# Feed-forward work listed in pieces of two blocks; pooled scores head by head, pooled products with V in blocks of 48 queries

## The chip, the core and the metric

The kernel runs on one core of a Trainium2 chip. The metric is the device time of one execution in microseconds (us); of several executions the median is taken. The core's engines run side by side, each through its own list of instructions in order: TensorE (PE; its weight loads are shown as PEld), VectorE (DVE), ScalarE (ACT), GpSimd (POOL), and SyncE (SP), which here issues every DMA.

## The reference

Eight sequences of 576 positions with 8 heads of 64 go through two attentions whose sum goes through a normalisation and a feed-forward layer of 2048 inner units; everything is float32.

```python
q_d = q.reshape(B, H, Sd, 4, D).mean(axis=3)          # Sd = 144; k_d, v_d alike
out_up = np.repeat(sm_attn(q_d, k_d, v_d), 4, axis=2)  # pooled attention, 144 x 144 scores a head
mask = np.abs(pos[:, None] - pos[None, :]) < 4
out_local = softmax(where(mask, scale * q @ k.T, -1e9)) @ v
x = (out_up + out_local)                               # 4608 rows of 512
xn = (x - mean) / sqrt(var + 1e-6) * g_ln
out = x + relu(xn @ w_ch1) @ w_ch2                     # 512 -> 2048 -> 512
```

## The kernel before

**Three streams of work.** The *local* attention takes 40 windows (5 a sequence), each with 8 heads: scores `ls` (L573, L587), a transpose of the attention `lt` (L622), products with V `lv` (L643). The *pooled* attention takes each sequence in two halves of four heads (`pooled_half`), each in two pairs of heads (`pooled_pair`): 32 pairs, of which the four of sequence 0 (`own`) have forms of their own. The *feed-forward* layer takes 18 chunks of 256 rows; the 2048 inner units are 8 pairs of two blocks of 128 (`ffn(c, p)`). For each block, `up(fi)` makes 12 matmuls into `h` (L1048) and `down(fi)` 6 into `acc` (L1071): inputs and weights are split into a high and a low float32r part, and three of the four products are kept. There are 288 `up` and 288 `down` pieces.

**A pooled pair before (not of sequence 0).** `turn_qk` transposes Q and K of both heads (`gq`, L791). `turn_qk_out` copies Q of each head into its own rows and columns of `qbdg`, a block-diagonal tile whose other parts stay zero, and K into `ktg` (L800, L804). `scores` then needs three matmuls, of 128 rows and 96 columns, 48 queries of both heads at once, over 144 keys (`gs`, L818). `largest` is one maximum over 96 x 432 and one small product on DVE (L822, L823), `exps` three activations (L831). `turn_a` transposes the attention in two halves of the keys, three transposes of 96 columns each (`gt`, L837), each copied out by `turn_a_out` (L847). `times_v` is eight matmuls of 72 x 72 by 65 columns (`gv`, L854), `divided` follows on DVE, and `keep` writes the result to DRAM in one DMA (L877).

**Array tiles.** Matmuls of `ls` and `lv` have 64 rows and 64 columns, and stand on four 64 x 64 tiles of TensorE's 128 x 128 array, those of L428 (sequence 0's transposes, `lq`, `lk`) on two tiles of 128 x 64. All other matmuls use the whole array.

**What sets the order.** Nothing is ordered by hand. Each piece of work is a task of `Plan`: engine, assumed duration, the tasks that it depends on, a due time, and the "rooms" (buffers, PSUM banks among them) that it takes and gives. A task is never split. `Plan.order` simulates the engines and, among the tasks that can start, takes the one that is due first. Due times follow a pace: chunk `c` is due at `T0 + CHUNK * c`, so `CHUNK` (56) scales the dues of attention too. The order that comes out is what each engine executes.

Of the kernel before, what the change touches and what calls it, by code (L numbers as in the profile page):

```python
# [139 lines left out]
def attention_then_ffn(  # L140
# [72 lines left out]
    qbdg = [const.tile([P, 3, 2 * GB], F32, name=f"qbdg{i}") for i in range(2)]  # L213
# [56 lines left out]

    T0 = 35
    C1 = 5
    CHUNK = 56
    PACE = CHUNK / NPR

    def chunk_at(c):
# [45 lines left out]
    def act(n, sbuf=False):  # L322
        return (0.155 if sbuf else 0.14) + n / 1430.0
# [404 lines left out]
    def pooled(b):  # L728
        due0 = pooled_at(b, 0)
        add = plan.add  # L730
        for hg in range(2):
            pooled_half(b, hg)

    def pooled_half(b, hg):
        add = plan.add
        i = 2 * b + hg
        x = SimpleNamespace(m={})
        vd = vds[hg]
        ready = {}
        own = b < NPB  # L740
        if own:
            ready["q"], ready["k"] = list(gsum_done[b, hg, "q"]), list(gsum_done[b, hg, "k"])
        for nm, src in (("v", v),) if own else (("q", q), ("k", k), ("v", v)):
            for half in range(2):
                key = (nm, half)
                due = pooled_at(b, 2 * hg) - (8.0 if nm == "v" else 14.0)
# [28 lines left out]
                ready.setdefault(nm, []).append(t)  # L775
        for pr in range(2):
            pooled_pair(b, hg, pr, x, ready)

    def pooled_pair(b, hg, pr, x, ready):
# [2 lines left out]
        due = pooled_at(b, 2 * hg + pr)  # L782
        y = SimpleNamespace(at={})
        own = b < NPB
        bd, vd = qbdg[pr], vds[hg]

        def turn_qk():
            y.pt = psa(f"gq{i}_{pr}")[:, : 2 * SD].rearrange("p (t g) -> p t g", t=2)
# [17 lines left out]
        def arrange():
            for h2 in range(2):
                hs = slice(64 * h2, 64 * h2 + 64)
                nc.scalar.copy(
                    bd[hs, :, h2 * GB : (h2 + 1) * GB],  # L810
                    gsum[b, hg, "q"][hs, pr].rearrange("p (c g) -> p c g", c=3),
                )
            y.kt = gsum[b, hg, "k"][:, pr]

        def scores():
            y.ps = psa(f"gs{i}_{pr}")[: 2 * GB, : 3 * SD].rearrange("p (c g) -> p c g", c=3)
            for c in range(3):
                nc.tensor.matmul(y.ps[:, c], lhsT=bd[:, c], rhs=y.kt, start=True, stop=True)  # L818

        def largest():  # L820
            y.mx = work.tile([2 * GB, 3], F32, tag="gmx", bufs=4, name=f"gmx{i}_{pr}")
# [18 lines left out]
                )  # L840

        def turn_a_out(kh):
            if own:
                y.at[kh] = unit([GH, 2, SD], f"agt{i}_{pr}_{kh}")
            else:
                y.at[kh] = work.tile([GH, 2, SD], F32, tag=f"agt{kh}", name=f"agt{i}_{pr}_{kh}")
            nc.scalar.copy(y.at[kh].rearrange("p h (c g) -> p c h g", c=3), y.pa[kh])  # L847

        def times_v():
            y.pv = psa(f"gv{i}_{pr}")[:GH, : 4 * (D + 1)].rearrange("p (q h e) -> p q h e", q=2, h=2)  # L850
            for h2 in range(2):
                for qh in range(2):
                    for kh in range(2):
                        nc.tensor.matmul(  # L854
                            y.pv[:, qh, h2], lhsT=y.at[kh][:, h2, qh * GH : (qh + 1) * GH],
                            rhs=vd[:, kh, 2 * pr + h2], start=kh == 0, stop=kh == 1,
                        )

        def divided():
            r = work.tile([GH, 2, 2], F32, tag="gr", bufs=4, name=f"gr{i}_{pr}")  # L860
# [19 lines left out]
            )  # L880

        if b < NPB:
            t = add("ACT", 0.43, arrange, ready["q"] + ready["k"] + [lastg.s[pr]], due - 8.0)
        else:
            t = add("PE", 0.25, turn_qk, ready["q"] + ready["k"], due - 8.0, take=A, give=(("u", 2),) if pr else ())
            t = add("ACT", 0.52, turn_qk_out, (t, lastg.s[pr]), due - 8.0, give=A)
        t = lastg.s[pr] = add(
            "PE", 0.73, scores, (t,), due - 6.0, take=A, give=(("u", 2),) if b < NPB and pr else ()
        )
        t = add("DVE", 0.7, largest, (t,), due - 5.0)  # L890
        ex = add("ACT", 0.79, exps, (t, None if own else lastg.t), due - 5.0, take=U if own else (), give=A)
        outs = []
        for kh in range(2):
            t = lastg.t = add("PE", 0.25, lambda kh=kh: turn_a(kh), (ex,), due - 3.0, take=A,
                                give=U if own and kh else ())
            outs.append(add("ACT", act(288), lambda kh=kh: turn_a_out(kh), (t, None if own else lastg.v), due - 3.0,
                            take=U if own else (), give=A))
        t = add("PE", 1.04, times_v, outs + ready["v"], due - 1.0, take=A, give=(("u", 2),) if own else ())
        lastg.v = lastg.vd[hg] = t
        t = add("DVE", 0.68, divided, (t,), due, take=U if b < NPB and pr == 0 else (), give=A)  # L900
        od_done.append(t)
# [134 lines left out]
    def ffn(c, p):  # L1036
# [48 lines left out]
            nc.sync.dma_start(out_f[n * P : (n + 1) * P], xt[n])  # L1085

        ups = []
        for fi in range(2):
            ups.append(
                add("PE", 1.44, lambda fi=fi: up(fi),  # L1090
                    xt_done[c] + [wdone[1, 2 * p + fi]] + ups[-1:] + [f1_last.get(c)], due + 0.1 * fi,
                    take=() if fi else A, give=rooms("xh", "xh", "xlo", "xlo") if p == NPR - 1 and fi else ())
            )
# [4 lines left out]
        for fi in range(2):  # L1098
            prev = add(
                "PE", 1.38, lambda fi=fi: down(fi), (t, wdone[2, 2 * p + fi], prev),  # L1100
                due + (2 * PACE if c < 2 else PACE) * (OFF0 if c < 2 else 2) + 0.1 * fi,
                take=(("a", TPC),) if p == 0 and fi == 0 else (), give=rooms("hh", "hl") if fi else (),
            )
        f2_done[c] = prev
        if p == NPR - 1:
# [65 lines left out]
```

## Time and profile before

| | us |
|---|---|
| Median of 3 runs | 1056.92 |
| Lowest, highest | 1055.81, 1063.01 |
| The profiled execution | 1053.27 |
| Its span, first to last instruction | 1051.3 |

| Engine | busy us | share of the span |
|---|---|---|
| PE | 1034.3 | 98% |
| PEld | 928.9 | 88% |
| DVE | 514.0 | 49% |
| ACT | 309.8 | 29% |
| POOL | 251.0 | 24% |

Matmuls are pipelined, and one that is recorded as 0.40 us long can be followed by the next after 0.23 us. So a busy PE tells little, and the cost of matmuls is read here from the **starts** in the timeline: from the start of a group to the start of what follows. In the timeline `64*64` stands for rows and columns of the array, `64x65` for what is written; a float32 matmul shows as two records, a transpose and a float32r matmul as one. A few per cent of the records are missing.

### The profile page before, as it was taken

The page shows a single profiled execution, that of the slowest core. Times are in us where ns is not written, and L with a number is a line of the kernel's source. Part 1 is how long each engine was busy: PE and PEld are TensorE (multiplying, and loading weights), DVE is VectorE, ACT ScalarE, POOL GpSimd, SP SyncE. Part 2 cuts the span into 40 slices and gives each one's busy share as a digit, 9 for nine tenths or more (in the row PEclk, how much of TensorE's full clock was granted, in tenths as well). Part 3 has the DMA queues.
Part 4 walks back from the last instruction along what each step waited for, and adds up shares of the span by engine and source line. Part 5 has one row for each costly group of instructions (what it writes and reads, how often), then busy time and mean ns, then how long its engine had stood idle before and what let it go on. Part 6 is the DMA issues. An engine that isn't in the chain of part 4 may idle for free.

```text
span 1051.3 us, 24104 instructions
## 1 busy us (share of the span) xinstructions
PE 1034.3 (98%) x9450; PEld 928.9 (88%) x9450; DVE 514.0 (49%) x1301; ACT 309.8 (29%) x846; POOL 251.0 (24%) x272
## 2 busy tenths in 40 slices
PE   9999899999999999999999999999999999999998
PEld 8887798988899989989898989899989899888997
DVE  7799976343444435444434443544434444534211
ACT  6676533232212222221323222222221222221110
POOL 4213552214014320231404150141401300000000
PEclk9999999999999999999999999999999999999999
DMA  7897474434344534343434443253442443301000
GB/s 177 251 283 210 136 176 95 114 64 114 61 101 91 133 75 110 62 124 56 91 94 96 104 97 99 47 134 67 114 87 69 92 88 65 80 11 52 7 21 21
DMA packets 283702, 104.38 MB, mean 99 GB/s; under 512 B 229789, under 2 KB 270493, under 8 KB 283589
## 3 DMA queue, kind: packets, MB, share of 16 engines
q1 hardware_dynamic: 283589, 102.84, 40.8%
q8 instruction: 75, 1.23, 0.5%
q14 instruction: 38, 0.31, 0.1%
HBM read 82.58 MB, written 11.80 MB: 90 GB/s over the span
## 4 chain that ended last, share of the span: by engine, by line
PE 83%; DVE 6%; DMA 5%; SPq 2%; issue 1%; POOL 1%; ACT 1%; ACTq 0%; DVEq 0%; POOLq 0%
PE h L1048 34%; PE acc L1071 33%; PE gv L854 3%; DMA s<-in_moe_w_ch_dram 2%; PE gs L818 2%; PE lv L643 2%; PE ls L587 2%; DVE cva L370 2%; PE lt L622 1%; PE px L975 1%; PE gt L837 1%; DVE lo L383 1%; SPq L714 1%; DMA x<-xl 1%; DVE cva L367 1%
## 5 line engine op out<-in xcount | busy, mean ns | idle before, releaser
L1071 PE MATMUL acc<-hi,hl 128*128 128x512 f32 x576 | 237.2, 412 | 0.6 <-DVE hl L1059 0.5
L1071 PE MATMUL acc<-lo,hh 128*128 128x512 f32 x576 | 227.4, 395 | 0.0
L1071 PE MATMUL acc<-hi,hh 128*128 128x512 f32 x576 | 225.2, 391 | 0.0
L1059 DVE SCALAR_TENSOR_TENSOR hl<-h,hh 128x512 fp32r<-128x512 f32 x144 | 98.9, 687 | 250.7 <-ACT hh L1055 222.0
L1055 ACT ACTIVATE hh<-h 128x512 fp32r<-128x512 f32 x144 | 86.2, 599 | 430.3 <-PE h L1048 363.5
L1048 PE MATMUL h<-xh,lo 128*128 128x256 f32 x1152 | 193.6, 291 | 0.2 <-DVE lo L383 0.2
L1048 PE MATMUL h<-xh,hi 128*128 128x256 f32 x1152 | 185.2, 283 | 0.0
L1048 PE MATMUL h<-xlo,hi 128*128 128x256 f32 x1152 | 185.0, 283 | 0.0
L1048 PEld LDWEIGHTS h<-xh,lo 128*128 128x128 f32 x1152 | 169.0, 190 | 17.4 <-DVE lo L383 0.4
L1048 PEld LDWEIGHTS h<-xlo,hi 128*128 128x128 f32 x1152 | 158.9, 192 | 0.0
L1048 PEld LDWEIGHTS h<-xh,hi 128*128 128x128 f32 x1152 | 158.6, 191 | 0.0
L948 POOL TENSOR_TENSOR x<-x,up 128x512 f32<-128x512 f32 x32 | 41.2, 1287 | 386.3 <-DMA x<-xl 208.1
L1071 PEld LDWEIGHTS acc<-hi,hh 128*128 128x128 f32 x576 | 108.5, 188 | 25.0
L1071 PEld LDWEIGHTS acc<-hi,hl 128*128 128x128 f32 x576 | 109.2, 190 | 16.9 <-DVE hl L1059 1.2
L1071 PEld LDWEIGHTS acc<-lo,hh 128*128 128x128 f32 x576 | 109.5, 190 | 12.7 <-DVE lo L383 0.3
L982 ACT ACTIVATE xh<-px,gain 128x128 fp32r<-128x128 f32 x144 | 43.7, 372 | 72.7 <-PE px L975 42.4
L992 DVE SCALAR_TENSOR_TENSOR xlo<-px,gain,xh 128x128 fp32r<-128x128 f32 x144 | 43.1, 345 | 39.1 <-ACT xh L982 38.6
L1079 DVE SCALAR_TENSOR_TENSOR x<-acc,x 128x512 f32<-128x512 f32 x36 | 24.7, 689 | 39.8 <-PE acc L1071 39.8
L831 ACT ACTIVATE ag<-gs,gmx 96x144 f32<-96x144 f32 x96 | 29.0, 374 | 41.9 <-DVE gmx L823 34.4
L370 DVE SCALAR_TENSOR_TENSOR cva<-s,cva 128x256 int32<-128x256 int32 x64 | 40.0, 665 | 1.1
L854 PEld LDWEIGHTS gv<-vd,agt 72*72 72x72 f32 x512 | 37.1, 145 | 1.2
L854 PE MATMUL gv<-vd,agt 72*72 72x65 f32 x512 | 37.9, 228 | 0.0
(196 smaller groups left out, 1106.9 us busy)
## 6 DMA issues: line engine op xcount, KB each, us to landing
s<-in_moe_w_ch_dram SPq DMA_DIRECT2D x64, 256.0 KB
vwin<-in_v_dram SPq DMA_DIRECT2D x160, 64.0 KB
out_dram<-x SPq DMA_DIRECT2D x36, 256.0 KB
qr<-in_q_dram SPq DMA_DIRECT2D x264, 32.0 KB
kr<-in_k_dram SPq DMA_DIRECT2D x264, 32.0 KB
up<-ud SPq DMA_DIRECT2D x28, 256.0 KB
x<-xl SPq DMA_DIRECT2D x74, 42.0 KB
ud<-od SPq DMA_DIRECT2D x32, 72.0 KB
```

The source lines that it names most:

```text
L370: nc.vector.scalar_tensor_tensor(out=a, in0=x.raw[i].rearrange("p (n two) -> p n two", two=2)[:, :, 0], scalar=29, in1=a, op0=ALU.logical_ ...
L587: nc.tensor.matmul(x.ps[par][64 * h2 : 64 * h2 + 64, pr], lhsT=x.qt[hs, 2 * pr + h2], rhs=x.kt[hs, 2 * pr + h2], start=True, stop=True,)
L831: nc.scalar.activation(y.a[:, c], y.ps[:, c], AF.Exp, scale=POOLED_SCALE, bias=y.mx[:, c : c + 1])
L854: nc.tensor.matmul(y.pv[:, qh, h2], lhsT=y.at[kh][:, h2, qh * GH : (qh + 1) * GH], rhs=vd[:, kh, 2 * pr + h2], start=kh == 0, stop=kh == 1,)
L948: nc.gpsimd.tensor_add(xt[n], xt[n], x.up)
L982: nc.scalar.activation(xh[c][i][:, k, j * P : (j + 1) * P], pxt[n][:, kc], AF.Copy, scale=gain[:, kc : kc + 1])
L992: nc.vector.scalar_tensor_tensor(out=xlo[c][i][:, k, ts], in0=pxt[n][:, kc], scalar=gain[:, kc : kc + 1], in1=xh[c][i][:, k, ts].bitcast(F ...
L1048: nc.tensor.matmul(ph[c, p][:, fi], lhsT=wt[:, kc], rhs=xx[kc // 2][:, kc % 2], start=n == 0, stop=n == 3 * KC - 1)
L1055: nc.scalar.activation(hh[c, p], ph[c, p], AF.Relu)
L1059: nc.vector.scalar_tensor_tensor(out=hl[c, p].rearrange("p c t -> p (c t)"), in0=ph[c, p].rearrange("p c t -> p (c t)"), scalar=0.0, in1=h ...
L1071: nc.tensor.matmul(acc[c][j], lhsT=lt[:, fi, ts], rhs=rt, start=p == 0 and fi == 0 and n == 0, stop=p == NPR - 1 and fi == 1 and n == 2,)
L1079: nc.vector.scalar_tensor_tensor(out=x, in0=acc[c][j], scalar=1.0 + 2.0**-23, in1=x, op0=ALU.mult, op1=ALU.add)
```

## The change

- **Feed-forward pieces.** For chunks 2 to 17, the two `up` pieces of a pair become one task (24 matmuls), and the two `down` pieces one (12 matmuls). Chunks 0 and 1 keep single pieces.
- **Pace.** `CHUNK` goes from 56 to 53.
- **Pooled scores by head** (sequences 1 to 7, 28 pairs): Q and K are copied in one activation. Each head then has its own three matmuls of 64 rows and 48 columns; the two heads stand on the diagonal 64 x 64 tiles and write two PSUM banks. The maximum, its product, the exponentials and the transposes are done once for each head: 2 maxima, 6 activations, 12 transposes of 48 columns on tiles of 64 x 128.
- **Products with V in blocks of 48 queries**: 12 matmuls instead of 8, on the two 128 x 64 column halves, one head on each. The first head's matmul takes 64 columns, so that the unused rows between the heads hold numbers too. The division works on 112 x 192 instead of 72 x 256; the result leaves in two DMAs of 256 B pieces instead of one of 512 B pieces.
- `qbdg` is still used by sequence 0; it is now cleared by a task (`clear_qbdg`) in buffers that are given back.

The core of the diff (dues, rooms and the scheduling of the pooled tasks follow from it):

```diff
-    CHUNK = 56
+    CHUNK = 53
...
+        def turn_qk_out_both():
+            y.qk = work.tile([P, 2, SD], F32, tag="ktg", bufs=2, name=f"ktg{i}_{pr}")
+            nc.scalar.copy(y.qk.rearrange("p t g -> p (t g)"), y.pt.rearrange("p t g -> p (t g)"))
+
+        def scores_by_head():
+            y.ps = [psa(f"gs{i}_{pr}_{h2}")[:, : 3 * SD].rearrange("p (c g) -> p c g", c=3) for h2 in range(2)]
+            for c in range(3):
+                for h2 in range(2):
+                    hs = slice(64 * h2, 64 * h2 + 64)
+                    nc.tensor.matmul(
+                        y.ps[h2][64 * h2 : 64 * h2 + GB, c], lhsT=y.qk[hs, 0, c * GB : (c + 1) * GB], rhs=y.qk[hs, 1],
+                        start=True, stop=True,
+                    )
...
+        def turn_a_by_head(h2):
+            hs = slice(64 * h2, 64 * h2 + GB)
...
+            for kh in range(2):
+                for c in range(3):
+                    n = (3 * kh + c) * GB
+                    nc.tensor.transpose(
+                        y.pa[h2][:, n : n + GB], y.a[hs, c, kh * GH : (kh + 1) * GH], ident[hs, hs]
+                    )
...
+        def times_v_by_third():
+            y.pv = psa(f"gv{i}_{pr}")[: 64 + GB, : 3 * (D + 1)].rearrange("p (c e) -> p c e", c=3)
+            for c in range(3):
+                for kh in range(2):
+                    for h2 in range(2):
+                        m = GB if h2 else 64
+                        c0 = (6 * h2 + 3 * kh + c) * GB
+                        nc.tensor.matmul(
+                            y.pv[64 * h2 : 64 * h2 + m, c], lhsT=y.at.rearrange("p h n -> p (h n)")[:, c0 : c0 + m], rhs=vd[:, kh, 2 * pr + h2],
+                            start=kh == 0, stop=kh == 1,
+                        )
...
+            t = lastg.qk[pr] = add("PE", 0.4, scores_by_head, (t,), due - 6.0, take=(("a", 2),))
+            exs = []
+            for h2 in range(2):
+                t1 = add("DVE", 0.78, lambda h2=h2: largest_by_head(h2), (t,), due - 5.0)
+                exs.append(add("ACT", 1.1, lambda h2=h2: exps_by_head(h2), [t1, lastg.t] + exs, due - 5.0, give=A))
...
-        t = add("PE", 1.04, times_v, outs + ready["v"], due - 1.0, take=A, give=(("u", 2),) if own else ())
+        t = add("PE", 1.04 if own else 0.5, times_v if own else times_v_by_third, outs + ready["v"], due - 1.0, take=A, give=(("u", 2),) if own else ())
...
-        for fi in range(2):
+        groups = ((0,), (1,)) if c < 2 else ((0, 1),)
+        for fs in groups:
             ups.append(
-                add("PE", 1.44, lambda fi=fi: up(fi),
+                add("PE", 1.44 * len(fs), lambda fs=fs: [up(fi) for fi in fs],
...
-                "PE", 1.38, lambda fi=fi: down(fi), (t, wdone[2, 2 * p + fi], prev),
+                "PE", 1.38 * len(fs), lambda fs=fs: [down(fi) for fi in fs],
...
+    bd_done = plan.add("DVE", 0.6, clear_qbdg, (), 0.0, take=(("u", 2),))
```

**Two places in the order of TensorE.** The first is the pooled scores of one pair in the middle of the program (sequence 4, second half, during chunk 7). Before, between a `down` piece (`acc`) and an `up` piece (`h`):

```order
L1071 MATMUL acc_1_6539<-hi_1_1284,hh_0_6491 128x512
L622 MATMUL lt_6613<-ident,la_6479 128x128 x4
L818 MATMUL gs_0_6624<-ktg_0_6597,qbdg_80 96x144 x3
L1048 MATMUL h_3_6630<-xh_0_6318,lo_6_1681 128x256 x2
L1048 MATMUL h_3_6630<-xh_1_6337,lo_6_1681 128x256 x2
L1048 MATMUL h_3_6630<-xh_0_6318,hi_6_1659 128x256 x2
```

Now, with `gs_0_0` and `gs_0_1` the two heads:

```order
L1123 MATMUL h_2_6822<-xlo_1_6594,hi_5_1563 128x256 x2
L620 MATMUL lt_6858<-ident,la_6767 128x128 x4
L810 MATMUL gs_0_0_6863<-ktg_0_6850 48x144
L810 MATMUL gs_0_1_6864<-ktg_0_6850 48x144
L810 MATMUL gs_0_0_6863<-ktg_0_6850 48x144
L810 MATMUL gs_0_1_6864<-ktg_0_6850 48x144
L810 MATMUL gs_0_0_6863<-ktg_0_6850 48x144
L810 MATMUL gs_0_1_6864<-ktg_0_6850 48x144
L1146 MATMUL acc_0_6873<-hi_0_1254,hl_0_6770 128x512
L1146 MATMUL acc_0_6873<-lo_0_1303,hh_0_6765 128x512
```

Three matmuls on the whole array have become six on two diagonal tiles, and what stands around them are pieces of double length.

The second place is the transposes of the same pair's attention (`gt`), before:

```order
L1071 MATMUL acc_1_6539<-lo_2_1452,hh_1_6547 128x512
L1071 MATMUL acc_1_6539<-hi_2_1440,hh_1_6547 128x512
L837 MATMUL gt_0_0_6703<-ident,ag_0_6670 72x96 x3
L837 MATMUL gt_0_1_6707<-ident,ag_0_6670 72x96 x3
L1071 MATMUL acc_0_6538<-hi_3_1456,hl_1_6566 128x512
L1071 MATMUL acc_0_6538<-lo_3_1490,hh_1_6547 128x512
```

Now (`gt_0_0` and `gt_0_1` were the halves of the keys, and are the heads now):

```order
L1123 MATMUL h_3_6928<-xlo_0_6544,hi_7_1710 128x256 x2
L1123 MATMUL h_3_6928<-xlo_1_6594,hi_7_1710 128x256 x2
L838 MATMUL gt_0_0_6965<-ident,ag_0_6922 72x48 x6
L838 MATMUL gt_0_1_6972<-ident,ag_0_6922 72x48 x6
L1146 MATMUL acc_0_6873<-hi_2_1477,hl_1_6852 128x512
L1146 MATMUL acc_0_6873<-lo_2_1485,hh_1_6847 128x512
```

Six transposes on the whole array have become twelve of half the columns on tiles of 64 x 128. Over the whole program, the runs of matmuls on tiles smaller than the array, between matmuls on the whole array, are 80 in the order before and 155 now.

## Rows read from the trace of the kernel before

**Rows 1.** The page, part 1: busy time, share of the span, instructions of each engine.

```profile
PE 1034.3 (98%) x9450; PEld 928.9 (88%) x9450; DVE 514.0 (49%) x1301; ACT 309.8 (29%) x846; POOL 251.0 (24%) x272
```

**Rows 2.** Stretches: length; busy time of PE, PEld, DVE, ACT, POOL; PEclk; DMA share; GB/s.

```profile
57.00:110.00 53.00, 50.52 (x434) 44.62 (x435) 51.83 (x106) 37.78 (x105) 16.42 (x15) 0.97 0.83 250
110.00:163.00 53.00, 48.84 (x348) 43.51 (x347) 45.69 (x83) 21.71 (x56) 30.29 (x27) 0.97 0.54 133
```

**Rows 3.** All waits of PE from 232 us to the end: total us, times, longest.

```profile
PE gs L818 <- DVE hl L1059: 1.4, 1, 1.4
```

**Rows 4.** Timeline of PE at 245 us: start, us, engine, line, operation, out<-in, forms, count.

```profile
245.49 0.39 PE L1071 MATMUL acc<-hi,hh 128*128 128x512 f32 x1
245.81 0.69 PE L587 MATMUL ls<-lkt,lqt 64*64 64x64 f32 x32
246.43 0.73 PE L1048 MATMUL h<-xh,lo 128*128 128x256 f32 x4
247.00 0.64 PE L1048 MATMUL h<-xh,hi 128*128 128x256 f32 x4
247.48 0.64 PE L1048 MATMUL h<-xlo,hi 128*128 128x256 f32 x4
247.96 0.40 PE L1071 MATMUL acc<-hi,hl 128*128 128x512 f32 x1
248.19 0.40 PE L1071 MATMUL acc<-lo,hh 128*128 128x512 f32 x1
```

**Rows 5.** Timeline of PE at 28 and 35 us: products with V of two windows, of one.

```profile
28.15 1.16 PE L643 MATMUL lv<-vwin,at 64*64 64x65 f32 x64
29.25 0.66 PE L622 MATMUL lt<-ident,la 128*128 128x128 f32 x4
...
34.98 0.70 PE L643 MATMUL lv<-vwin,at 64*64 64x65 f32 x32
35.60 0.66 PE L622 MATMUL lt<-ident,la 128*128 128x128 f32 x4
```

**Rows 6.** Timeline of PE at 254 us: pooled transposes, pooled scores.

```profile
254.03 0.29 PE L791 MATMUL gq<-ident,qd 72*128 72x72 f32 x2
254.16 0.29 PE L791 MATMUL gq<-ident,kd 72*128 72x72 f32 x2
...
257.98 0.90 PE L818 MATMUL gs<-ktg,qbdg 128*96 128x144 f32 x6
258.62 0.49 PE L1071 MATMUL acc<-hi,hl 128*128 128x512 f32 x1
```

**Rows 7.** Timeline of PE at 231 us: pooled attention transposed; pooled products with V.

```profile
231.44 0.66 PE L837 MATMUL gt<-ident,ag 96*72 96x96 f32 x6
231.88 0.47 PE L1071 MATMUL acc<-hi,hl 128*128 128x512 f32 x1
...
233.35 1.19 PE L854 MATMUL gv<-vd,agt 72*72 72x65 f32 x16
234.36 0.72 PE L1048 MATMUL h<-xh,lo 128*128 128x256 f32 x4
```

**Rows 8.** Timeline of PE at 7 and 16 us: transposes on two column halves.

```profile
6.67 0.72 PE L428 MATMUL lq<-ident,qo 80*64 80x80 f32 x16
7.23 0.72 PE L428 MATMUL lk<-ident,ko 80*64 80x80 f32 x16
...
16.64 0.72 PE L428 MATMUL lk<-ident,ko 80*64 80x80 f32 x16
17.30 0.98 PE L818 MATMUL gs<-gsk,qbdg 128*96 128x144 f32 x6
```

**Rows 9.** Groups of DVE: busy us, mean ns | idle before, releaser.

```profile
L822 DVE TENSOR_REDUCE gmx<-gs 96x3 f32<-96x432 f32 x32 | 19.2, 600 | 25.6 <-PE gs L818 25.6
L823 DVE TENSOR_SCALAR gmx<-gmx 96x3 f32<-96x3 f32 x32 | 6.9, 216 | 1.1
```

**Rows 10.** Groups of ACT: the same columns.

```profile
L831 ACT ACTIVATE ag<-gs,gmx 96x144 f32<-96x144 f32 x96 | 29.0, 374 | 41.9 <-DVE gmx L823 34.4 <-PE acc L1071 7.5
```

More of the change, by code (lines that the diff above doesn't have):

```diff
@@ L212, in attention_then_ffn @@
     vwins = [const.tile([P, 2, NPAIR, D + 1], F32, name=f"vwin{i}") for i in range(NVW)]
-    qbdg = [const.tile([P, 3, 2 * GB], F32, name=f"qbdg{i}") for i in range(2)]
+    qbdg = []
     vds = [const.tile([GH, 2, 4, D + 1], F32, name=f"vd{i}") for i in range(2)]
@@ L732, in pooled, with clear_qbdg @@
             pooled_half(b, hg)
+    def clear_qbdg():
+        for pr in range(2):
+            qbdg.append(unit([P, 512], f"qbdg{pr}")[:, : 6 * GB].rearrange("p (c g) -> p c g", c=3))
+            nc.vector.memset(qbdg[pr], 0.0)
     def pooled_half(b, hg):
@@ L784, in pooled_pair @@
         own = b < NPB
-        bd, vd = qbdg[pr], vds[hg]
+        vd = vds[hg]
         def turn_qk():
@@ L806, in arrange, with turn_a_out_by_head @@
+        def turn_a_out_by_head(h2):
+            if h2 == 0:
+                y.at = work.tile([GH, 2, 6 * GB], F32, tag="agt", name=f"agt{i}_{pr}")
+            nc.scalar.copy(y.at[:, h2], y.pa[h2])
         def arrange():
@@ L809, in arrange @@
                 nc.scalar.copy(
-                    bd[hs, :, h2 * GB : (h2 + 1) * GB],
+                    qbdg[pr][hs, :, h2 * GB : (h2 + 1) * GB],
                     gsum[b, hg, "q"][hs, pr].rearrange("p (c g) -> p c g", c=3),
@@ L817, in scores @@
             for c in range(3):
-                nc.tensor.matmul(y.ps[:, c], lhsT=bd[:, c], rhs=y.kt, start=True, stop=True)
+                nc.tensor.matmul(y.ps[:, c], lhsT=qbdg[pr][:, c], rhs=y.kt, start=True, stop=True)
         def largest():
@@ L842, in turn_a_out @@
         def turn_a_out(kh):
[L843 to L846, printed above, removed]
+            y.at[kh] = unit([GH, 2, SD], f"agt{i}_{pr}_{kh}")
             nc.scalar.copy(y.at[kh].rearrange("p h (c g) -> p c h g", c=3), y.pa[kh])
@@ L882, in pooled_pair @@
         if b < NPB:
-            t = add("ACT", 0.43, arrange, ready["q"] + ready["k"] + [lastg.s[pr]], due - 8.0)
+            t = add("ACT", 0.43, arrange, ready["q"] + ready["k"] + [lastg.s[pr], bd_done], due - 8.0)
         else:
             t = add("PE", 0.25, turn_qk, ready["q"] + ready["k"], due - 8.0, take=A, give=(("u", 2),) if pr else ())
[L886 to L889, printed above, removed]
@@ L890, in pooled_pair @@
-        t = add("DVE", 0.7, largest, (t,), due - 5.0)
-        ex = add("ACT", 0.79, exps, (t, None if own else lastg.t), due - 5.0, take=U if own else (), give=A)
+            t = add("ACT", 0.36, turn_qk_out_both, (t, lastg.qk.get(pr)), due - 8.0, give=A)
+        if own:
+            t = lastg.s[pr] = add("PE", 0.73, scores, (t,), due - 6.0, take=A, give=(("u", (2 if pr else 0) + hg),) if pr or hg else ())
+            t = add("DVE", 0.7, largest, (t,), due - 5.0)
+            exs = [add("ACT", 0.79, exps, (t,), due - 5.0, take=U, give=A)]
+        else:
+            t = lastg.qk[pr] = add("PE", 0.4, scores_by_head, (t,), due - 6.0, take=(("a", 2),))
+            exs = []
+            for h2 in range(2):
+                t1 = add("DVE", 0.78, lambda h2=h2: largest_by_head(h2), (t,), due - 5.0)
+                exs.append(add("ACT", 1.1, lambda h2=h2: exps_by_head(h2), [t1, lastg.t] + exs, due - 5.0, give=A))
@@ L892, in pooled_pair @@
         outs = []
         for kh in range(2):
-            t = lastg.t = add("PE", 0.25, lambda kh=kh: turn_a(kh), (ex,), due - 3.0, take=A,
+            t = lastg.t = add("PE", 0.25, lambda kh=kh: turn_a(kh) if own else turn_a_by_head(kh), exs if own else [exs[kh]], due - 3.0, take=A,
                                 give=U if own and kh else ())
-            outs.append(add("ACT", act(288), lambda kh=kh: turn_a_out(kh), (t, None if own else lastg.v), due - 3.0,
+            outs.append(add("ACT", act(288), lambda kh=kh: turn_a_out(kh) if own else turn_a_out_by_head(kh), (t, None if own else lastg.v), due - 3.0,
@@ L897, in pooled_pair @@
                             take=U if own else (), give=A))
-        t = add("PE", 1.04, times_v, outs + ready["v"], due - 1.0, take=A, give=(("u", 2),) if own else ())
+        t = add("PE", 1.04 if own else 0.5, times_v if own else times_v_by_third, outs + ready["v"], due - 1.0, take=A, give=(("u", 2),) if own else ())
         lastg.v = lastg.vd[hg] = t
-        t = add("DVE", 0.68, divided, (t,), due, take=U if b < NPB and pr == 0 else (), give=A)
+        t = add("DVE", 0.6, divided if own else divided_by_third, (t,), due, take=U if b < NPB and pr == 0 else (), give=A)
@@ L901, in pooled_pair @@
         od_done.append(t)
-        t = add("SP", 0.42, keep, (t,), due, lag=LAT)
+        t = add("SP", 0.42 if own else 0.84, keep if own else keep_by_third, (t,), due, lag=LAT)
         ud_done.setdefault(b, []).append(t)
@@ L1097, in ffn @@
         prev = f2_done.get(c)
-        for fi in range(2):
+        for fs in groups:
             prev = add(
-                "PE", 1.38, lambda fi=fi: down(fi), (t, wdone[2, 2 * p + fi], prev),
-                due + (2 * PACE if c < 2 else PACE) * (OFF0 if c < 2 else 2) + 0.1 * fi,
-                take=(("a", TPC),) if p == 0 and fi == 0 else (), give=rooms("hh", "hl") if fi else (),
+                "PE", 1.38 * len(fs), lambda fs=fs: [down(fi) for fi in fs],
+                [t, prev] + [wdone[2, 2 * p + fi] for fi in fs],
+                due + (2 * PACE if c < 2 else PACE) * (OFF0 if c < 2 else 2) + 0.1 * fs[0],
+                take=(("a", TPC),) if p == 0 and 0 in fs else (), give=rooms("hh", "hl") if 1 in fs else (),
             )
```

43 lines of the change are left out of this document (32 added, 11 removed).

## The prediction

> **What bounds the kernel now.** I read the page first: PE is busy 98% of the span, no other engine half of it [rows 1]. Busy time of pipelined matmuls can hide holes, so I asked next for PE's waits: from 232 us to the end there is a single one of note, 1.4 us [rows 3]. From 57 to 163 us PE is not busy for 2.5 + 4.2 = 6.6 us and its granted clock has a mean of 0.97, at which 106 us lose 3.2 us; DVE is busy 97.5 of those 106 us, with the conversion of the weights [rows 2]. So for three quarters of the time the kernel is as long as its list of matmuls, and in one tenth DVE is nearly as full as PE. A change is worth what it does to the list of PE.
>
> **How I price matmuls.** From start to start. Within feed-forward work four `up` matmuls take 0.48 us (247.00 to 247.48), one `down` matmul 0.23 us, and going from `h` to `acc` costs nothing (247.48 to 247.96 is 0.48 too) [rows 4]. Work on small tiles is different. The last `acc` starts at 245.49 and could be followed at 245.72, yet `ls` starts at 245.81: 0.09 us to enter. The four `h` behind it take 0.57 instead of 0.48: 0.09 us behind it [rows 4]. And leaving costs: two `lv` in a row take 1.10 us (28.15 to 29.25), one alone 0.62 (34.98 to 35.60), so the second adds 0.48 and the other 0.14 us is paid once, before anything else can start [rows 5]. A visit to small tiles therefore costs 0.09 + 0.14 + 0.09 = 0.32 us beside its matmuls.
>
> **What is removed**, for each of the 28 pairs. `gs`: 257.98 to 258.62, 0.64 us [rows 6]; `gt`: 231.44 to 231.88, 0.44; `gv`: 233.35 to 234.36, 1.01 [rows 7]. Each also delays the feed-forward matmuls behind it, by about the 0.09 us read behind `ls`: 0.73 + 0.53 + 1.10 = 2.36 us, times 28 = 66.1 us.
>
> **What is added**, without visits. *Scores*: twelve records, two heads side by side, so six steps of the same 144 columns as before: 0.73 us, 20.4 us in all. *Products with V*: 24 records in two column halves. `lq` has 16 records of 80 columns in two halves and takes 0.56 us (6.67 to 7.23) [rows 8], 0.035 us a record; for 65 columns 0.028, times 24 = 0.68 us, 19.1 us in all. *Transposes*: twelve of 48 columns, which no row shows. Half of a `gt` before (0.44 / 6 = 0.073) is 0.037 us [rows 7]; two `gq` of 72 columns take 0.13 us, 0.065 each [rows 6]. These are the bounds; I take 0.05, nearer to the proportional one since cost followed columns elsewhere: 0.60 us, 16.8 us in all (12.3 to 21.8). Sum 56.3 us, so the matmuls themselves get cheaper by 9.8 us.
>
> The Trainium skill speaks for more here: "TensorE: Matmul & The Clock Gate", section LDWEIGHTS (loading the stationary operand), has a weight load last its columns divided by 1.2 GHz. By it the 72 columns of each new transpose would load for 60 ns, an estimate, and the sum would be 3.4 us higher. The trace disagrees: `gq` loads 128 columns each time and follows itself after 65 ns, where the page would give 107; I keep the row.
>
> **Visits.** In the order of PE, the runs on small tiles between runs on the whole array are 80 before and 155 after: 29 are `gt` alone, 23 `gv` alone, 21 `gs` alone, and only few join `ls` or `lv`. 75 more visits at 0.32 us are 24.0 us. Inside visits the tile shape changes 15 times more; I charge each the 0.14 us of leaving: 2.1 us. So the account of PE is -9.8 + 24.0 + 2.1 = **+16.3 us** (11.8 to 21.3 by the bounds of the transposes).
>
> The Trainium skill states in "TensorEngine Tiling (Array Packing)", Key Properties, that changing the tiling mode, and not merely the tile, drains TensorE. The trace agrees for 64 x 64, with the 0.14 us above. By that rule 64 x 128 and 128 x 64 pay as well, as in my sum; if only 64 x 64 paid, the sum would be that of the first rival.
>
> **The joined pieces and the pace** add and remove no instruction. A border between two feed-forward pieces costs nothing, so joining them saves nothing; what joining could save, small-tile visits that meet, is in the count of 155. A joined piece holds PE for 2.9 us, which delays others' work by as much; the one PE wait after 232 us [rows 3] says that work stands ready early enough, so I charge nothing. If that cover goes, it is the last rival.
>
> **What other engines get.** DVE makes the maximum and its product twice: 0.600 + 0.216 = 0.82 us more a pair [rows 9], 23 us on an engine that is half idle; only from 57 to 163 us is there no cover. Five pairs stand there before the last weight in DVE's order, 4.1 us. PE grows there by the same pairs, so both stretch together; I take 1 us (0 to 4). ACT has three more exponentials, 29.0 / 96 = 0.30 us each [rows 10], 25 us on an engine with 71% idle; the copies get fewer. Both lengthen the chain of a pair by 1.7 us before its transposes, with feed-forward work on PE meanwhile. SP issues 28 more DMAs of smaller pieces, and nobody on PE waits for them. The clearing of `qbdg` only moves on DVE ahead of work that waits for inputs.
>
> **The sum.** +16.3 + 1 = +17.3 us. On the profiled execution's 1053.27 that is 1070.6; that execution lies 3.7 us below the median of 1056.92, so for the median I say **1074 us**, 1.6% slower.
>
> **Rivals.**
> *The new tile shapes change for nothing.* Then the 52 visits of `gt` or `gv` alone cost nothing (-16.6 us), nor do the 15 changes (-2.1): 17.3 - 18.7 = -1.4, 1055.5 us, no change. For it: no row shows 64 x 128. Against it: `lk` on 128 x 64 takes 0.66 us (16.64 to 17.30) where `lq` took 0.56 [rows 8], so leaving that shape costs 0.10. It decides within 1% once a visit costs under 0.23 us on the mean (75 visits x 0.23 - 9.8 + 2.1 + 1 = 10.6 us).
> *The early holes close.* Another order and pace could give back all of the 6.6 us of holes and 3.2 us of clock between 57 and 163 us: 17.3 - 9.8 = +7.5, 1064 us, still within 1%. Against it: DVE is full there [rows 2] and gets more work.
> *The diagonal tiles do not run side by side.* Then the scores take twelve steps, +0.73 us a pair, 20.4 us: 1095 us. Against it: the second `lv` has 32 records of 65 columns in 0.48 us, 0.015 each [rows 5], and a record of 72 columns on the whole array takes 0.065 [rows 6]: tiles do overlap.
> *PE begins to wait in the middle.* Scores now take two of eight PSUM banks until both heads' exponentials are done, the chain is longer, and pieces are twice as long. Half a microsecond a pair is 14 us: 1088 us. For it: the planner assumes 0.4 us for the new scores and 0.5 for the new products, where I expect 1.05 and 1.0 with a visit. Against it: a slower PE gives the others more time.
>
> **How the numbers follow.** Forecast 0.70, free shapes 0.10, holes closed 0.08, PE waits 0.07, no overlap 0.05. The likeliest case gives 1074. Its own range is 11.8 + 0 to 21.3 + 4 us, 1069 to 1082. For 8 times in 10 I go from 1057, short of the free shapes, to 1090, past the waits and short of the case without overlap. A measurement of this kernel can tell about 1% from no change, so the border lies at 1067.5 and 1046.4. The bounds are estimates, so 0.12 of the forecast's 0.70 falls short of 1067.5 and 0.58 is slower. Of the 0.18 of free shapes and closed holes I give 0.06 to both together, 17.3 - 18.7 - 9.8 = -11.2 us, 1045.7, just faster by 1%; the other 0.12 is no change. The waits and the missing overlap are slower. So: slower 0.58 + 0.07 + 0.05 = 0.70, same 0.12 + 0.12 = 0.24, faster 0.06.
>
> **What would show it.** In the new profile: the span grows with PE still at 98% and DVE, ACT still far below; `gs` to its successor about 0.87 us and `gv` 0.82, with 0.09 us before and behind each; a `gt` of both heads about 0.74 us. Right on visits: after 232 us PE has no more waits, yet ends later. Wrong: starts that follow `gt` or `gv` without 0.14 us; `gs` of 1.5 us; a new wait of PE for ACT's exponentials or copies; fewer holes before 163 us.

## The result, and the profile after

| | median us (runs) | profiled execution, its span | visits to small tiles |
|---|---|---|---|
| before | 1055.28 (20) | 1053.27, 1051.3 | 80 |
| after | 1064.14 (20) | 1062.39, 1060.3 | 155 |

The ratio is 1.0081 with the interval 1.0062 to 1.0100: the change makes the kernel 0.8% slower, by 8.9 us of median and 9.0 us of span. That lies inside the range of 1057 to 1090, below the likeliest case's own range of 1069 to 1082, and within 1%, where the prediction had 1074 us and 1.6%. The sign was right, the size is half. Single executions of one kernel lie far apart, 1050.6 to 1063.0 us for before and 1060.6 to 1068.9 for after, so an account of two profiled executions to a tenth of a microsecond is an account of these two.

The page of after, its part 1 and two groups (line, engine, operation, out<-in, form, count | busy, mean ns | idle before). They answer [rows 1, 9, 10]:

```profile
PE 1042.9 (98%) x10034; PEld 918.9 (87%) x10034; DVE 533.6 (50%) x1351; ACT 331.2 (31%) x898; POOL 249.9 (24%) x272
...
L827 ACT ACTIVATE ag<-gs,gmx 48x144 f32<-48x144 f32 x168 | 50.9, 369 | 31.9 <-DVE gmx L820 30.4
L819 DVE TENSOR_REDUCE gmx<-gs 48x3 f32<-48x432 f32 x56 | 33.8, 603 | 33.3 <-PE gs L810 32.5
```

PE is still busy 98%, DVE and ACT half and less. DVE's maxima went from 19.2 to 33.8 us, ACT's exponentials from 29.0 to 50.9 us, each instruction as long as before. Hardly any wait came of it: all waits of PE from 232 us to the end (total us, times, longest) are these, 1.9 us where before has the 1.4 us of [rows 3]:

```profile
PE lt L620 <- ACT la L611: 1.4, 1, 1.4
PE px L1050 <- DVE xn L1041: 0.5, 1, 0.5
```

**Where the 9 us arise.** I split both executions at 232 us and counted what PE still had to do. Groups of PE from 232 us on, before (the columns as in the groups above, the last number is the idle time):

```profile
L1071 PE MATMUL acc<-hi,hl 128*128 128x512 f32 x490 | 200.8, 410 | 0.0
L1071 PE MATMUL acc<-lo,hh 128*128 128x512 f32 x490 | 193.2, 394 | 0.0
L1071 PE MATMUL acc<-hi,hh 128*128 128x512 f32 x490 | 191.3, 390 | 0.0
L1048 PE MATMUL h<-xh,lo 128*128 128x256 f32 x960 | 160.3, 289 | 0.0
...
L854 PE MATMUL gv<-vd,agt 72*72 72x65 f32 x352 | 26.3, 227 | 0.0
...
L818 PE MATMUL gs<-ktg,qbdg 128*96 128x144 f32 x126 | 19.0, 287 | 1.4 <-DVE hl L1059 1.4
```

The same of after:

```profile
L1146 PE MATMUL acc<-hi,hl 128*128 128x512 f32 x491 | 200.3, 408 | 0.0
L1146 PE MATMUL acc<-lo,hh 128*128 128x512 f32 x491 | 192.2, 391 | 0.0
L1146 PE MATMUL acc<-hi,hh 128*128 128x512 f32 x491 | 192.0, 391 | 0.0
L1123 PE MATMUL h<-xh,lo 128*128 128x256 f32 x960 | 161.2, 290 | 0.0
...
L906 PE MATMUL gv<-vd,agt 72*64 72x65 f32 (+1 forms) x528 | 20.1, 225 | 0.0
L810 PE MATMUL gs<-ktg 64*48 64x144 f32 x252 | 19.6, 288 | 0.0
```

At 232 us the two kernels stand at the same place. Left are 490 or 491 of each `acc`, 960 of each `h`, the scores of 21 pairs (126 / 6 and 252 / 12) and the products with V of 22 (352 / 16 and 528 / 24). After is behind by three `acc` of 0.23 us and by the transposes of one pair (264 / 12 = 22 left, where before has 21): 1.2 us. In these two executions the 7 pairs ahead of 232 us, a quarter of the change, cost next to nothing. From there to the end before takes 1051.3 - 232 = 819.3 us and after 1060.3 - 232 = 828.3: nearly all of the 9.0 us is paid by the other 21 pairs, 7.8 us once the 1.2 us are taken off, or 0.37 us a pair.

**Ahead of 232 us.** Stretches of before (length, busy us of PE, PEld, DVE, ACT, POOL, then the granted clock, DMA share and GB/s):

```profile
91.30:94.50 3.20, 3.07 (x37) 2.56 (x38) 3.13 (x10) 2.32 (x8) 0.00 (x0) 0.50 0.76 184
132.30:135.50 3.20, 3.20 (x16) 3.20 (x16) 3.17 (x5) 0.91 (x2) 1.92 (x2) 0.50 1.02 206
224.40:227.60 3.20, 2.85 (x13) 2.84 (x14) 1.71 (x4) 0.92 (x4) 0.00 (x0) 0.50 0.51 121
57.00:232.00 175.00, 166.25 (x1403) 148.13 (x1404) 129.11 (x272) 81.05 (x230) 63.10 (x58) 0.97 0.59 154
```

And of after:

```profile
57.00:232.00 175.00, 166.25 (x1522) 144.61 (x1521) 132.21 (x286) 86.25 (x238) 61.98 (x59) 1.00 0.61 158
```

PE is busy the same 166.25 of 175 us in both, so its pauses did not get shorter: they sum to 8.75 us in each. What differs is the clock. Before runs three stretches of 3.4 us at half clock (granted 0.50, 1.2 of 2.4 GHz; the rows show 3.2 us of each), 3 x 1.7 = 5.1 us lost; each comes with a pause of PE that waits for ACT (2.2, 2.1 and 1.3 us). After has none until its last microseconds. A pause alone doesn't explain a drop, since after pauses as long and keeps 1.00:

```profile
83.77 0.71 PE L1123 MATMUL h<-xh,lo 128*128 128x256 f32 x4 [2.52 <-DVE lo L381]
...
143.88 0.45 PE L838 MATMUL gt<-ident,ag 48*72 48x48 f32 x6 [1.50 <-DVE gr L913]
```

It is tempting to say that after did its additional work in the time that before lost to the clock. The other executions speak against it as a rule. The mean granted clock of after over its 20 executions is 0.997 (0.993 to 1.000), that of before over the 47 timed beside the experiments 0.996 (0.991 to 0.999). Taking the span times what the clock lacks of 1, an estimate, after loses 3.5 us on average and before 4.5. The 5.1 us belong to these two executions, and after's profiled one, with 0.999, is near the top.

### The profile page after: what moved, and what is told of

Same layout as the page of the kernel before. It is cut to its first block, busy times and chain, and to the rows that moved or that the text cites. A ratio compares the mean times of both kernels' runs of the same rounds, so it can differ in the third digit from the quotient of the medians.

```text
span 1060.3 us, 25406 instructions
## 1 busy us (share of the span) xinstructions
PE 1042.9 (98%) x10034; PEld 918.9 (87%) x10034; DVE 533.6 (50%) x1351; ACT 331.2 (31%) x898; POOL 249.9 (24%) x272
## 4 chain that ended last, share of the span: by engine, by line
PE 90%; DVE 4%; DMA 3%; issue 1%; SPq 1%; ACT 1%; POOL 0%; ACTq 0%; POOLq 0%
PE h L1123 38%; PE acc L1146 36%; PE lv L641 2%; PE gv L906 2%; PE gs L810 2%; PE ls L585 2%; PE lt L620 2%; PE gt L838 2%; PE px L1050 1%; DMA s<-in_moe_w_ch_dram 1%; DVE lo L381 1%; DVE cva L368 1%; DMA raw2k<-in_k_dram 1%; PE gq L794 1%; DVE cva L365 1%
## 5 line engine op out<-in xcount | busy, mean ns | idle before, releaser
L1123 PEld LDWEIGHTS h<-xh,lo 128*128 128x128 f32 x1152 | 160.9, 191 | 12.6 <-issue 4.2
L827 ACT ACTIVATE ag<-gs,gmx 48x144 f32<-48x144 f32 x168 | 50.9, 369 | 31.9 <-DVE gmx L820 30.4
L819 DVE TENSOR_REDUCE gmx<-gs 48x3 f32<-48x432 f32 x56 | 33.8, 603 | 33.3 <-PE gs L810 32.5
L591 DVE TENSOR_TENSOR ls<-ls,mask 128x256 f32<-128x256 f32 x66 | 26.5, 425 | 25.4 <-PE ls L585 25.3
L647 DVE TENSOR_SCALAR lr<-lv 128x4 f32<-128x4 f32 x80 | 11.8, 147 | 54.6 <-PE lv L641 54.3
L913 DVE TENSOR_SCALAR gr<-gv 112x3 f32<-112x3 f32 x28 | 4.5, 159 | 66.4 <-PE gv L906 66.4
```

Of the source, the lines that this page charges most:

```text
L591: nc.vector.tensor_add(x.ps[n], x.ps[n], mask.unsqueeze(1).broadcast_to([P, NPAIR, 64]))
L819: nc.vector.reduce_max(y.mx[hs], y.ps[h2][hs], axis=AX.X)
L827: nc.scalar.activation(y.a[hs, c], y.ps[h2][hs, c], AF.Exp, scale=POOLED_SCALE, bias=y.mx[hs, c : c + 1])
L1123: nc.tensor.matmul(ph[c, p][:, fi], lhsT=wt[:, kc], rhs=xx[kc // 2][:, kc % 2], start=n == 0, stop=n == 3 * KC - 1)
```

## The experiments

Each ratio is to the kernel before, timed beside it.

**Joined pieces alone**, the kernel before with this edit:

```diff
-        for fi in range(2):
+        groups = ((0,), (1,)) if c < 2 else ((0, 1),)
+        for fs in groups:
...
```

> The kernel before, with the feed-forward pieces of chunks 2 to 17 joined and nothing else changed (pace 56, pooled work as before). Theory A (the new pooled forms cost TensorE about 14 us, and joined pieces with the new pace give back about 5 by closing early holes): joined pieces alone -2 to -4 us, 80 visits to small tiles as before, less time not busy between 57 and 163 us than the 6.6 us of before. Rival B (the new pooled forms cost only the 9 us that were measured, the rest changes nothing): 0 us, within 1 us.

Measured: 1048.30 us, ratio 0.9950 (0.9924 to 0.9976), span 1046.3: 5 us faster than before, more than the 2 to 4 expected, and the fastest kernel here. The groups of `acc` from 232 us on:

```profile
L1071 PE MATMUL acc<-hi,hl 128*128 128x512 f32 x484 | 196.6, 406 | 0.0
L1071 PE MATMUL acc<-lo,hh 128*128 128x512 f32 x484 | 189.5, 392 | 0.0
L1071 PE MATMUL acc<-hi,hh 128*128 128x512 f32 x485 | 189.4, 390 | 0.0
```

Seventeen fewer than before: at 232 us it is 17 x 0.23 = 3.9 us ahead, with one half-clock stretch instead of three, which is 3.4 us. PE's idle time up to 163 us, which I expected to shrink, is 6.5 us and was 6.6. Only the other 1.1 us are gained later. There the feed-forward work is interrupted 143 times instead of 163; at the 0.1 us that the first matmul behind an interruption takes longer, 20 fewer would be 2 us, an estimate of which half is seen. Waits take nothing of it: they are 1.4 us in both. So joining does not save borders, as I had said; that it saves interruptions is likely, not shown.

**The pace alone**, and **both without the pooled part**:

```diff
-    CHUNK = 56
+    CHUNK = 53
```

> The kernel before, with the pace 53 for 56 and nothing else changed. Theory A: -1 to -3 us, by a granted clock without drops between 57 and 232 us. Rival B: 0 us, within 1 us. If the pace is what hurt (attention due earlier, in the stretch where DVE is full): +2 to +4 us.

> The kernel before, with joined pieces and the pace 53, pooled work as before. Theory A: -5 us (from -3 to -7), holes and clock loss before 232 us shrink by about that. Rival B: 0 us, within 1 us.

Measured: the pace alone 1076.49 us, 1.0207 (1.0166 to 1.0247); both 1065.19, 1.0127 (1.0087 to 1.0167). Waits of PE with the pace alone, from 232 us:

```profile
PE px L975 <- DVE xn L966: 10.8, 2, 6.0
PE gs L818 <- ACT ktg L804: 2.8, 2, 1.5
PE lt L622 <- ACT la L613: 2.1, 1, 2.1
```

These are 15.7 us where before has 1.4, and 10.2 us at half clock behind them add 5.1. With both parts, 12.2 us of such waits remain. I had charged the pace nothing, and expected a gain from it in both runs.

**The pooled part alone** (single pieces, pace 56, the rest of the diff as it is):

> The kernel before with the pooled change alone: scores by head, products with V in blocks of 48 queries, single feed-forward pieces, pace 56. It has 160 visits to small tiles where the kernel before has 80. Theory A: +12 to +16 us, nearly all of it on TensorE after 232 us. Rival B: +9 us.

Measured: 1066.13 us, 1.0116 (1.0082 to 1.0149), with 160 visits: +12.5 us on its own, inside what was expected. The profiled execution is the longest of its six. What PE has left there from 232 us on begins so:

```profile
L1146 PE MATMUL acc<-hi,hl 128*128 128x512 f32 x492 | 202.3, 411 | 0.0
...
L1123 PE MATMUL h<-xh,lo 128*128 128x256 f32 x964 | 162.7, 291 | 0.0
```

That is six `acc` and twelve `h` more than before over the three products each, and beside them 32 `lv`, five `px` and the transposes of one pair: some 4 us behind, an estimate from the times above. So here the early pairs are not free, and not nearly all of the loss arises after 232 us.

**The whole change with one part taken back**: the pace at 56, or the pieces single.

> The changed kernel with the pace 56 put back; joined pieces and the new pooled forms stay (153 visits to small tiles, 155 in the changed kernel). Theory C (the three parts do not add up: the pace 53 costs 18 to 22 us beside the old pooled forms, but nothing beside the new ones, whose assumed durations are shorter): +12.3 for the pooled forms and -5.3 for the joined pieces, so +7 us against the kernel before (from +5 to +10). Rival D (the pace costs as much here as there): -9 us or better, since the measured +8.5 would hold 18 us of pace.

> The changed kernel with single feed-forward pieces in all chunks; pace 53 and the new pooled forms stay (158 visits). Theory C: joined pieces are worth 5 us here too, so +13 to +14 us against the kernel before. Rival E (joined pieces are worth something only by the holes that they happen to close in one order): +8 to +10 us.

Measured: with the pace at 56, 1063.99 us, 1.0111 (1.0087 to 1.0134), 11 us where 7 were expected from adding the parts, and about what the change has (1.0081): beside the new pooled forms the pace costs nothing that these runs can tell, though it costs 23 us beside the old. At 232 us this run has 488 of each `acc` left, where joined pieces alone have 484 or 485, and 32 `lv`, eight `px` and the transposes of one pair more: the pooled forms are again some 4 us behind, and the joined pieces again some 4 us ahead, so the two cancel. With single pieces 1075.27, 1.0220 (1.0193 to 1.0246), well past both expectations, so the joined pieces are worth 1.4% here, nearly three times as much as alone. Its profiled execution (1070.07) is the shortest of its five, so it shows only part of that. Of the 7.8 us between the two profiled executions I can name 7.1: 0.5 at 232 us, a wait of PE of 4.8 us on `px` where after waits 1.9 in all, 1.7 at half clock behind it, and 18 more interruptions, about 2. The parts do not add up: 12.5 - 5.4 + 22.8 is not 8.9, since each order has its own waits.

**What one visit costs, in an order that stays as it is.** The kernel before with one more matmul on one 64 x 64 tile behind each of the 28 pooled scores; its result is not used.

```diff
...
+            if not own:
+                nc.tensor.matmul(bank[:64, 3 * SD : 3 * SD + 64], lhsT=y.kt[:64, :64], rhs=y.kt[:64, :64], start=True, stop=True)
```

> The kernel before, with one more matmul of 64 x 64 by 64 columns behind the pooled scores of each of the 28 pairs, into 64 columns of their PSUM bank that nobody reads: the price of a visit by itself, 108 visits instead of 80, every other instruction in the same place. Theory C (each visit costs its entering, leaving and what follows): two records one behind the other 0.11 us, leaving 0.14, entering 0.09, and the 0.09 us that the scores save when a feed-forward piece follows: 0.43 us, +12 us (from +10 to +13). Rival H (a visit costs only its matmuls, the rest is hidden in other waits): 28 times 0.11, +3 us.

Measured: 1063.58 us, 1.0111 (1.0087 to 1.0135), +10.6 us of median and +8.2 of span. Timeline of PE (start, us, engine, line, operation, out<-in, forms, count, [idle before <-releaser]):

```profile
222.82 0.94 PE L622 MATMUL lt<-ident,la 128*128 128x128 f32 x4 [0.28 <-ACT la L617]
224.61 0.98 PE L819 MATMUL gs<-ktg,qbdg 128*96 128x144 f32 x6 [0.85 <-ACT ktg L804]
225.52 0.33 PE L821 MATMUL gs<-ktg 64*64 64x64 f32 x2
225.77 0.66 PE L978 MATMUL px<-ident,xn 128*128 128x128 f32 x4
...
509.39 0.90 PE L819 MATMUL gs<-ktg,qbdg 128*96 128x144 f32 x6
510.22 0.33 PE L821 MATMUL gs<-ktg 64*64 64x64 f32 x2
510.47 0.50 PE L1074 MATMUL acc<-hi,hl 128*128 128x512 f32 x1
```

From `gs` to `acc` it is now 1.08 us (509.39 to 510.47) where it was 0.64 [rows 6]: 0.44 for the visit and its two records. This is the clearest run on the price. At 232 us it has 488, 489 and 489 `acc` left, four fewer than before, so in this execution its 7 early visits cost nothing; from there it takes 8.2 us longer, 9.1 with the four `acc`, which is 0.43 for each of 21 visits. Whether the early visits are free in general it does not settle: the medians differ by 10.6 us (9.2 to 14.2 by the interval), where 21 visits at 0.43 are 9.0 and all 28 are 12.0. A place ahead of 232 us in before reads:

```profile
222.96 0.94 PE L622 MATMUL lt<-ident,la 128*128 128x128 f32 x4 [1.25 <-ACT la L617]
224.75 1.75 PE L818 MATMUL gs<-ktg,qbdg 128*96 128x144 f32 x6 [0.85 <-ACT ktg L804]
226.29 1.06 PE L975 MATMUL px<-ident,xn 128*128 128x128 f32 x4
```

With the visits PE comes to `lt` later and waits 0.28 us for ACT instead of 1.25, `lt` starts no later, and the half clock at which `gs` and `px` take 1.75 and 1.06 us in before does not come: `px` starts 0.5 us earlier than before although there is more to do ahead of it. This stretch of the visits' kernel, with its clock, and an earlier one, where it runs at half clock for twice as long as before does anywhere, with a pause of 2.95 us:

```profile
218.00:232.00 14.00, 12.86 (x116) 11.03 (x116) 9.44 (x28) 7.57 (x27) 2.54 (x3) 1.00 0.39 80
103.40:110.00 6.60, 5.79 (x23) 5.15 (x24) 5.78 (x11) 3.60 (x12) 3.08 (x2) 0.50 0.80 224
```

**The new scores without the new products with V**: the pooled part with `times_v` on the whole array, as before.

```diff
-                    for h2 in range(2):
-                        m = GB if h2 else 64
-                        c0 = (6 * h2 + 3 * kh + c) * GB
...
+            for h2 in range(2):
+                for qh in range(2):
...
```

> The kernel with the pooled change alone (single pieces, pace 56), but with the products with V on the whole array again: eight matmuls of 72 x 72, one DMA out. Scores and transposes stay by head, the planner's assumed durations stay, so the order does too; 139 visits instead of 160. Theory C (from the trace of the changed kernel: 0.84 us and a visit's 0.2 for the new products, 1.00 and 0.08 for the old ones): the blocks of 48 queries gain next to nothing, so this one is 0 to 3 us above the kernel with the whole pooled change, +12 to +15 us against the kernel before. Rival I (the blocks of 48 queries cost a good part of the loss): +6 to +9 us.

Measured: 1071.49 us, 1.0179 (1.0156 to 1.0202), 139 visits: +18.5 us, past both expectations. It is 0.6% slower than the whole pooled part, so the blocks of 48 queries seem to be a gain of some 6 us. But each ratio has its own timing of before, and from 232 us on the two profiled executions, the whole pooled part first, take about the same time for the same work (836.8 and 835.2 us, with 1.4 us more feed-forward work and 29 more `lv` left in the first). How much the blocks give stays open.

**Fewer visits.** Both heads' transposes as one task (the whole change otherwise), and, on the joined pieces alone, a planner that prefers local work on 64 x 64 tiles in a row:

```diff
+            both = lastg.t = add("PE", 0.5, lambda: [turn_a_by_head(h2) for h2 in range(2)], exs, due - 3.0, take=(("a", 2),))
...
```

```diff
+                few = sum(c[1].small for c in near) < 2
+                r, t = min(near, key=lambda c: (c[1].due + (20.0 * (few - 2 * was_small) if c[1].small else 0.0), c[1].n))
...
```

> The changed kernel with the transposes of both heads as one task of TensorE (28 runs of twelve; in the changed kernel 22 runs of six and 17 of twelve), 147 visits instead of 155. In the trace of the changed kernel six transposes alone take 0.375 us and twelve take 0.497. Theory F (the second head's transposes run beside the first's on the other row half): 11 times 0.375 + 0.20 - 0.12 = 0.45 us, -5 us against the changed kernel, so +4 us against the kernel before. Rival G (only the visits are saved): 8 times 0.33, -2.6 us, +6 us against the kernel before.

> The kernel before with joined pieces (pace 56, pooled work as before), and the planner prefers to run two local tasks on 64 x 64 tiles (scores of a window, products with V of a window) one behind the other: a lone one is put back by up to 20 us of due time. 58 visits instead of 80. If a visit costs 0.32 us wherever it stands: 22 times 0.32, -7 us against joined pieces alone, -12 us against the kernel before. If the delay makes others wait: 0 to +10 us against joined pieces alone, with new waits of TensorE after 232 us.

Measured: 147 visits, 1069.71 us, 1.0164 (1.0138 to 1.0191); and 58 visits, 1090.11 us, 1.0356 (1.0331 to 1.0381). Fewer visits made both slower, the first where a gain on the whole change was expected, the second by more than the 10 us on joined pieces that I had allowed for. In the first, the stretch from 57 to 232 us:

```profile
57.00:232.00 175.00, 161.49 (x1446) 140.57 (x1444) 133.12 (x268) 79.16 (x216) 62.32 (x56) 0.98 0.58 151
```

Its largest waits of PE there:

```profile
PE acc L1150 <- DVE hl L1138: 4.4, 2, 3.2
PE gs L810 <- ACT ktg L802: 4.3, 1, 4.3
```

PE is idle for 13.5 us there, where it was 8.75: the time is lost where PE waits for DVE and ACT. In the second PE waits 30.8 us from 232 us on, the longest being:

```profile
PE gq L798 <- POOL kd L773: 7.2, 1, 7.2
```

Work that is put back until it meets its like is late for those who wait for it; 22 visits at 0.33 us are 7 us, and the waits are more.

**Joined pieces, tuned**: pace 58, or durations nearer to the measured ones (0.82 us for local scores and products, 1.09 for pooled products).

> The kernel before with joined pieces and the pace 58 (joined at 56: -5.3 us, at 53: +13). Theory J (a pace faster than TensorE can follow makes the holes after 232 us): no such holes, -3 to -7 us against the kernel before. Rival K (the holes are an accident of each order): anything from -7 to +13 us, and holes in other places.

> The kernel before with joined pieces at pace 56, and the planner told what the trace shows of three tasks: 0.82 us for the scores and for the products of a window instead of 0.75 and 0.70, 1.09 us for the pooled products instead of 1.04. No instruction changes, only the order. Theory J: -5 to -8 us against the kernel before. Rival K: -7 to +13 us.

Measured: 1057.34 us, 1.0047 (1.0015 to 1.0079), and 1049.28 us, 0.9979 (0.9959 to 0.9998). With the joined pieces, pace 53, 56 and 58 give 1.0127, 0.9950 and 1.0047. Truer durations remove every wait of PE after 232 us, and the time is not better than with joined pieces alone: what it had to lose there was 1.4 us. The expectation that a pace which TensorE can follow leaves no such waits fails: at 58 there are 5.0 us of them.

## Why the prediction was half right

**Sign and mechanism: right.** The forecast was a PE list that grows through visits, with PE at 98%, the other engines far below, and no waits that take over. All of this is seen from 232 us on. The timeline of PE after:

```profile
296.13 0.57 PE L838 MATMUL gt<-ident,ag 48*72 48x48 f32 x12
296.62 0.50 PE L1146 MATMUL acc<-hi,hl 128*128 128x512 f32 x1
296.96 0.39 PE L1146 MATMUL acc<-lo,hh 128*128 128x512 f32 x1
...
299.58 0.91 PE L906 MATMUL gv<-vd,agt 72*64 72x65 f32 x24
300.43 0.74 PE L1123 MATMUL h<-xh,lo 128*128 128x256 f32 x4
301.00 0.64 PE L1123 MATMUL h<-xh,hi 128*128 128x256 f32 x4
...
319.37 0.64 PE L1123 MATMUL h<-xlo,hi 128*128 128x256 f32 x4
319.94 0.94 PE L810 MATMUL gs<-ktg 64*48 64x144 f32 x12
320.81 0.50 PE L1146 MATMUL acc<-hi,hl 128*128 128x512 f32 x1
321.14 0.39 PE L1146 MATMUL acc<-lo,hh 128*128 128x512 f32 x1
...
448.72 0.45 PE L838 MATMUL gt<-ident,ag 48*72 48x48 f32 x6
449.09 0.66 PE L1050 MATMUL px<-ident,xn 128*128 128x128 f32 x4
```

- *Scores*: 0.87 us to the successor (319.94 to 320.81), as forecast to the hundredth; so the diagonal tiles do run side by side. *Products with V*: 0.85 (299.58 to 300.43), forecast 0.82.
- *A visit*: entering takes 0.57 - 0.48 = 0.09 us (319.37 to 319.94); behind it `acc` takes 0.33 instead of 0.23 and `h` 0.57 instead of 0.48, so 0.09 to 0.10; with the 0.14 of leaving 0.33, forecast 0.32. Of this the 0.09 behind is not peculiar to small tiles: in before `acc` takes 0.31 behind `gt` on the whole array (231.88 to 232.19), as the prediction had charged on both sides. The run with the extra visits confirms it with 0.43 a visit, its two records included. The rival of free shapes falls with that. The Trainium skill's "TensorEngine Tiling (Array Packing)", Key Properties, has every change of the tiling mode drain TensorE; the trace fits that for 64 x 128 too, by the 0.37 us that six short transposes take to their successor, below; for 128 x 64 it has the 0.85 us of the products, where 0.68 without leaving and 0.82 with it were forecast.
- *Transposes*: **mis-sized.** I took 0.60 us a pair. Twelve take 0.49 us to the successor (296.13 to 296.62), six alone 0.37 (448.72 to 449.09). With 0.14 for leaving, six take 0.23, 39 ns each, and the second head's six only 0.12 more, 20 ns each, both estimates: the heads lie in different row halves and overlap, which I had expected of the scores but not here. Eleven pairs run as two visits of six (0.46) and 17 as one of twelve (0.35): 0.39 a pair, so 0.2 us a pair or 5.8 us too much, and 1.3 us below my lower bound of 12.3 us for all. The Trainium skill's rule in "TensorE: Matmul & The Clock Gate", section LDWEIGHTS (loading the stationary operand), that a load of 72 columns lasts 60 ns, an estimate from that page, would have led further away: the trace has 39 and 20.

**The steps that failed.** The first is the term of the transposes, "I take 0.05, nearer to the proportional one", 0.60 us a pair: it gave the two heads no overlap. They take 0.39 a pair, and that is 5.8 of the 8.3 us between the forecast of +17.3 and the 9.0 of the two spans. The second is "PE grows there by the same pairs, so both stretch together; I take 1 us", the charge for the early pairs: it is the rest, 2.5 us.

Late, 21 pairs: three quarters of my -9.8 and +2.1 us is -5.8, and 56 of the visits (116 instead of 60 from 232 us on) at 0.32 are 17.9: +12.1. Transposes at their measured price take off 21 x 0.2 = 4.2, which leaves 7.9; measured 7.8. That it closes to a tenth is partly luck: the pooled part alone has 60 more visits there, and the same count with its waits and clock gives some 10 us, where its profiled execution takes some 13.

Early: 4.2 + 1 = 5.2 us forecast, 3.8 with transposes at their measured price, and 1.2 measured in these two executions. DVE's share was far off: its last weight was converted 12 us later (173.6 instead of 161.6 us), where I had 4.1 us of delay in its list. Still the feed-forward work stood at the same place at 232 us. Why stays open. The rival of the closing holes, to which I gave 0.08, holds for the clock of these two executions and not for the holes: PE's idle time up to 163 us grew from 6.6 to 106 - 97.25 = 8.75 us. And with the pace at 56 the pooled forms do cost some 4 us early, about what I charged; it is the joined pieces that give as much back.

**"The joined pieces and the pace ... I charge nothing": not borne out.** The joined pieces are worth 5 us alone and 1.4% within the change, and the pace costs 2% beside the old forms. The count of 155 visits holds little of this: with single pieces it is 158, 1 us more. Without the joined pieces the change would be 2.2% slower. That the sum came out within 9 us owes something to luck, since these parts have opposite signs.

**What stays open**: why the pace of 53 makes late waits with the old pooled forms and none with the new. The orders show that it does; a rule that says beforehand which order will wait I have not found.

## What to carry to other kernels

Price a change to the bounding engine stage by stage, and count both executions' remaining work at one moment to see in which stage its cost arises. Before naming the cause, see whether other executions of the same kernels have the same clock. Smaller matmul tiles save their array time only if they come in few visits, since each visit costs a third of a microsecond here beside its matmuls. When a change has several parts, try each alone: here the joined pieces are a gain that the rest of the change covers up, and the kernel before with them alone is the fastest here.

## What the runs showed of the hardware

- Transposes of 48 columns follow each other after some 39 ns; those of the other row half fit between them at some 20 ns each (estimates from 0.37 us for six and 0.49 for twelve, 0.14 of it for leaving).
- A single matmul on a 64 x 64 tile between matmuls on the whole array costs 0.43 us, while 32 records of `ls` on such tiles take 0.62 us together (245.81 to 246.43, [rows 4]).
- In before, half-clock stretches (granted 0.50) of 3.4 us came with pauses of PE of 2.2, 2.1 and 1.25 us, and each cost 1.7 us; with the extra visits one of some 6.8 us came with a pause of 2.95 us. In after, pauses of 2.52, 1.50 and 1.31 us left the clock at 1.00. At one place (222 us) the drop went away when more work stood in the pause.
- The mean granted clock of single executions of one kernel ranged from 0.991 to 0.999 in before and from 0.993 to 1.000 in after.
